# Attention and a two-layer network on one core: the first 700 items of a hand-written order rearranged

## The chip, the core and the metric

The kernel runs on one core of a Trainium2 chip. The core has five engines, each with its own in-order queue: TensorE (matmul, PE in the profile; its weight loads are PEld), VectorE (DVE), ScalarE (ACT), GpSimd (POOL) and SyncE (SP), which here only issues DMAs. They wait for one another through semaphores. TensorE writes into PSUM, which has 8 banks of 128 x 512 float32. The metric is the device time of one execution in microseconds (us).

## What is computed

Attention with causal masks over 4 batches, 8 heads, 768 positions and 64 columns per head. Three heads see all earlier positions; the other five see the first 4 positions and a window of 64. The result, as 3072 tokens of 512 columns, goes through two matrix products with a leaky rectifier between them.

```python
scores = scale * np.matmul(q, k.transpose(0, 1, 3, 2))
...
stream_keep = causal & (is_sink | in_win)
...
a = np.exp(scores)
a = a / (np.sum(a, axis=-1, keepdims=True) + 1e-09)
return np.matmul(a, v).astype(np.float32)
```

```python
h = x @ w_in
g = np.maximum(h, 0.0) + alpha * np.minimum(h, 0.0)
return (g @ w_out).astype(np.float32)
```

w_in is 512 x 2048, w_out is 2048 x 512; x is the attention's result, batch by batch.

## The kernel before

**Segments and blocks.** The heads go in pairs (2,6), (1,5), (0,4), (3,7); a pair of one batch is a segment, n = 0 to 15, four to a batch. The first four (batch 0) are the first stage. The tokens go through the network in eight groups, t = 0 to 7: of each batch 512 tokens (even t) and 256 (odd t).

**Items.** The program is a list of some 1,100 named items, ORDER, which line 807 emits one after another. An item is one step of one segment or block; its letter tells which, and its numbers the segment (n), the head of the pair (h) and the part:

- Lq, Lk, Lv n: loads of q, k and v, on SyncE (one load of k on ScalarE, one on GpSimd). Cq, Ck, Cv: casts to bfloat16, on GpSimd, VectorE or ScalarE as strings at line 296 and below say.
- Tq, Tk n: transposes on TensorE into PSUM; tq, tk n.h: copies from there into qT and kT (put_q, line 369; put_k, line 387 and below). From segment 8 on DMAs do this (Dq, Dk).
- S n.h.m: scores of one part (TensorE, line 414 in the first stage; from segment 4 on they are gathered in a group and issued at lines 424 or 431, the two heads side by side). s n.h.m: exponentials (ScalarE, lines 470, 518, 524). m n.h.m: masks (VectorE, lines 480, 529, 532).
- A n.h: product with v (TensorE, line 553); a n.h: reciprocal and scaling (VectorE, lines 563 and 564). X n and x n: transposes into xT, by TensorE and VectorE (lines 578 and 583) in segments 0 to 3 and 15, by DMA (line 572) in the others.
- P t.f: the first product, 128 x 512 values of one bank (TensorE, line 598); in t = 0, blocks f < 6, it comes in three parts, the first of which reads the pairs 0 and 1 of xT. p t.f: negated rectifier (ScalarE, line 603, three buffers); g t.f: the rectifier's sum (VectorE, line 610), which frees the bank.
- O t.s.u: a quarter of the second product (TensorE, line 618); o t.s: copy out of PSUM (ScalarE, line 624) and the output's DMA (GpSimd, line 628). L and l are the last tile of it, in three cuts.
- Fills and masks that are made once: ro, sz, so, near (constants in the tails of the exponentials' buffers), kz, qz, vz, vo, nz, kfz (line 288 in the profile), nmr, nms (masks of the first stage, on GpSimd), nr, ns, one, zero, busy, id. warm: matmuls on the tile busy, without a use of their result (line 688).
- wi, wo: loads of the weights, issued by GpSimd.

**What sets the order.** An engine executes its own instructions in the order of the list; between engines only the data order them. The place in the list decides one more thing: a step that needs a PSUM bank takes, of those that its kind may use, the one that was given back longest ago in the list (take and give, lines 144 and 150), and so waits for whoever gave it back. Scores of the first stage take the banks 0 and 1 or 2 and 3 in pairs; A, X and some transposes of the first stage take 6 or 7; most others any.

**Names in the prediction.** tk0.1 is the copy of the second head's keys of segment 0 into kT, in two pieces (put_k, line 387); S0.1.0, S0.1.1 and S0.1.2 are that head's scores, s0.1.x their exponentials, A0.0 and A0.1 the products with v of the two heads. ro0 fills the tail of the first buffer eR, which A0.0 and A0.1 read. near2 refills parts of the third buffer eS. x1 copies the second pair's transposes into xT. m9.0.2 is two instructions (lines 529 and 532). nz0 zeroes a buffer that Ck8 writes into; Cv5 and Cv4 are casts of v on GpSimd.

Of the kernel before, what the change touches and what calls it, by code (L numbers as in the profile page):

```python
# [11 lines left out]


ORDER = """
vz2 id busy warm4 warm0 warm5 vz0 qz0 Lq0.0 sz2 so2 Lq0.1 zero vz3 nms Lk1 Lq1 sz1 Cq0.1 nmr Ck1.1 kz1 La Lk0 Ck1.0
kz0 Cq1 Cq0.0 Tq0.0 Ck0.0 Tk0.0 tk0.0 Lk2 Ck2.0 Lv0 warm2 tq0.0 S0.0.0 s0.0.0 qz S0.0.1 Tk1 warm3 warm6 vo kz2 Ck0.1
vz1 Ck2.1 Tq1 s0.0.1 tq1 Tq0.1 tk1.1 S0.0.2 s0.0.2 Cv0 tk1.0 m4.0.2 warm7 tq0.1 Lq2 S1.1.0 Tk0.1 tk0.1 S1.0.0 ro0
s1.1.0 Tk2 tk2.1 idf Cq2 s1.0.0 S0.1.0 s0.1.0 A0.0 S0.1.1 s0.1.1 S0.1.2 Tq2 warm8 s0.1.2 tq2 S1.1.1 s1.1.1 A0.1 kz3
sz0 Lk3 Ck3.1 Lv1 S1.0.1 m4.1.2 a0.0 s1.0.1 Al Ck3.0 Lq3 tk2.0 Tk3 S2.0.1 s2.0.1 a0.1 tk3.1 al X0 x0 S2.0.2 Lv2 Lv3
so1 so0 Lq5 wi1 s2.0.2 Lk4 m8.0.2 wi0 Cq3 Tq3 S2.0.0 s2.0.0 tk3.0 Cv1 tq3 A1.0 a1.0 Lk5 kfz2 A1.1 a1.1 kfz0 S2.1.0  # L20
S2.1.1 Cv2 s2.1.1 kfz3 wi6 A2.0 a2.0 wi7 S3.1.0 s2.1.0 s3.1.0 wi5 wi4 S3.0.0 A2.1 Cv3.0 s3.0.0 X1 S3.1.1 s3.1.1 S3.0.1
a2.1 X2 x1 x2 m8.1.2 near2 Ck4.0 P0.0.0 wi2 s3.0.1 A3.0 Cv3.1 P0.3.0 a3.0 P0.2.0 P0.2.1 A3.1 Ck4.1 Lk7 Lk6 P0.1.0
P0.1.1 P0.0.1 Tk4 tk4.0 Cq5 m14.0.2 a3.1 X3 nz1 tk4.1 x3 Tq5 P0.3.1 tq5 P1.2 p1.2 P1.0 p1.0 g1.0 P0.1.2 wi3 P0.13 Lq4
one p0.1 g0.1 P0.2.2 Lq6 Lv7 p0.2 P0.0.2 P1.14 p1.14 g1.2 g1.14 Ck5.0 Ck5.1 nr Tk5 tk5.1 P0.3.2 tk5.0 g0.2 p0.0 g0.0
p0.3 g0.3 P0.12 p0.12 g0.12 p0.13 g0.13 P0.14 kfz1 P1.8 P0.8 wo0 p0.8 g0.8 P0.10 Ck7.1 S5.1.1 s5.1.1 P0.15 p0.15 wo1
wo2 wo3 ns p1.8 g0.15 g1.8 P0.11 p0.11 p0.14 g0.14 p0.10 S5.0.0 Lv5 P0.7 g0.10 P0.6 Ck6.1 P0.4.0 Lq7 P0.4.1 Lk8 Ck6.0
s5.0.0 p0.7 S5.0.2 s5.0.2 Cq4 Tq4 tq4 g0.11 P0.4.2 P0.9 nz0 Ck7.0 S5.1.0 p0.9 g0.9 P1.4 s5.1.0 p1.4 Lv6 S4.0.1 Cq6
m12.1.2 P0.5.0 s4.0.1 P0.5.1 P0.5.2 P1.12 m5.0.0 g1.4 S4.0.3 g0.7 p0.4 p0.5 m5.1.0 g0.4 g0.5 Cv5 P1.10 S5.0.1 p1.10
s5.0.1 near0 p0.6 g0.6 O0.1.0 Tq6 s4.0.3 m4.0.3 Tk6 tk6.1 tk6.0 O0.2.0 P1.6 p1.6 m5.0.1 Tk7 tk7.1 Lv4 S4.0.2 O0.2.1
g1.6 ro1 tq6 p1.12 s4.0.2 tk7.0 O0.1.1 O0.2.2 O0.1.2 g1.10 S4.0.4 S4.0.0 S5.1.2 g1.12 S4.0.5 S4.1.4 S4.1.0 s4.0.4  # L30
s4.0.0 m5.1.1 m4.0.4 s4.1.0 m4.1.0 m5.0.2 O0.1.3 s5.1.2 O0.3.0 O0.2.3 Cq7 m5.1.2 Ck8 Tq7 near1 A5.1 o0.1 S6.1.0 s4.1.4
s6.1.0 O0.3.1 a5.1 s4.0.5 O0.3.2 O0.3.3 m4.0.1 m4.0.5 Cv4 tq7 S7.0.0 S6.0.5 S7.1.1 S4.1.1 Lk9 Lk10 Lq9 o0.2 o0.3
S4.1.3 S7.0.1 A5.0 s4.1.1 s7.0.0 m4.0.0 a5.0 X5 A4.0 s7.0.1 Lk11 s7.1.1 a4.0 s4.1.3 O1.1.0 m4.1.3 Cv7 s6.0.5 m7.0.0
m7.1.1 Lq8 S7.1.0 S6.0.4 S7.0.2 S4.1.5 S6.0.1 S7.1.2 S6.1.1 O1.1.1 Cv6 s7.1.0 O1.0.0 s4.1.5 m7.0.1 s6.1.1 m4.1.5
m6.1.1 s7.1.2 m6.1.0 s7.0.2 m7.0.2 S6.0.2 S4.1.2 S6.1.2 S6.0.0 s6.0.4 s4.1.2 s6.0.1 s6.1.2 O1.0.1 m6.0.5 m7.1.0 m4.1.1
# [812 lines left out]
```

## Time and profile before

| | us |
|---|---|
| median of the runs (227.71, 228.17, 228.29) | 228.17 |
| the profiled execution | 228.43 |
| its span, first to last instruction | 225.8 |
| TensorE busy | 221.6 |
| VectorE busy | 149.1 |
| ScalarE busy | 140.1 |
| GpSimd busy | 45.9 |

By stretches of the span, from the view that sums them (busy time of TensorE, VectorE, ScalarE and GpSimd):

| stretch, us | what runs | TensorE | VectorE | ScalarE | GpSimd |
|---|---|---|---|---|---|
| 0 to 26 | loads, first stage | 24.63 | 20.29 | 18.47 | 18.63 |
| 26 to 53 | first blocks P, segments 4 and 5 | 27.00 | 19.89 | 22.62 | 13.65 |
| 53 to 80 | segments 4 to 7, products O | 27.00 | 18.26 | 18.27 | 3.49 |
| 80 to 120 | blocks of batch 1, segments 8 to 11 | 40.00 | 32.41 | 30.59 | 4.30 |
| 120 to 225.8 | the rest | 102.92 | 58.30 | 50.12 | 5.87 |

In the rows of a timeline the columns are the start, the duration, the engine, the line, the operation, what is written and read with the shape, the count, and in brackets the idle time of the engine before it and what ended that. Neighbours of one kind are merged into one row with their count. Matmuls are pipelined: a matmul's duration reaches past the start of the next one, so the distance between starts tells the pace, and a busy TensorE can hold short waits. In the view of waits, the columns are who waited for what, the time in total, the number of waits and the longest. The chain is the work that ended last, followed back through what released each step; a row of it has start, duration, engine, tile and line.

### The profile page before, as it was taken

Reading aid. Unit: us, or ns where it says so; the run is one execution under the profiler, and the core shown is the slowest. Engines: PE = TensorE matmul, PEld = TensorE weight load, DVE = VectorE, ACT = ScalarE, POOL = GpSimd, SP = SyncE. Lnnn points to the kernel's source line nnn. Section 1 sums busy time; section 2 is a strip of 40 time slices with the busy share of each in tenths; the row PEclk is TensorE's granted clock in tenths of the full one; section 3 lists DMA queues with packets and bytes.
Section 4 is the critical chain, followed back from the end, with each engine's and each line's share of the span. In section 5 each row is a group of like instructions: output and inputs, shape, how many; then the busy total and the mean of one; then the engine's idle time right before and its main releaser. Section 6 shows DMA issues by size and latency. Waiting matters only on the chain.

```text
span 225.8 us, 5241 instructions
## 1 busy us (share of the span) xinstructions
PE 221.6 (98%) x2005; PEld 136.5 (60%) x2005; DVE 149.1 (66%) x393; ACT 140.1 (62%) x286; POOL 45.9 (20%) x91
## 2 busy tenths in 40 slices
PE   7999999999999999999999999999999999999994
PEld 7989876575556557564556455456556555664454
DVE  5798648986659618897899029977486536866000
ACT  3788669999898036587992147786584237563311
POOL 5679749600230001000400001000110100000000
PEclk9999999999999999999999999999999999999999
DMA  6999999999999999999989999976924420000213
GB/s 201 311 240 214 281 223 285 197 196 231 204 284 182 117 232 231 170 167 190 268 160 177 226 243 129 238 156 117 119 94 38 120 93 0 0 3 1 93 68 119
DMA packets 95417, 37.39 MB, mean 166 GB/s; under 512 B 82440, under 2 KB 93600, under 8 KB 95392
## 3 DMA queue, kind: packets, MB, share of 16 engines
q1 hardware_dynamic: 89136, 27.73, 65.2%
q0 software_dynamic: 5792, 8.93, 17.5%
q10 hardware_dynamic: 464, 0.40, 0.6%
q8 instruction: 15, 0.25, 0.5%
q14 instruction: 10, 0.08, 0.1%
HBM read 27.71 MB, written 6.29 MB: 151 GB/s over the span
## 4 chain that ended last, share of the span: by engine, by line
PE 98%; DVE 0%; issue 0%; DVEq 0%
PE P L598 37%; PE P L618 36%; PE P L553 7%; PE P L431 4%; PE P L414 3%; PE P L688 3%; PE P L364 2%; PE P L637 2%; PE P L424 1%; PE P L502 1%; PE P L578 1%; PE P L463 0%; PE P L362 0%; DVE kT L387 0%; DVE ot L646 0%
## 5 line engine op out<-in xcount | busy, mean ns | idle before, releaser
L610 DVE SCALAR_TENSOR_TENSOR g<-neg,oma,P 128x256 bf16<-128x256 f32 (+1 forms) x128 | 70.9, 608 | 36.9 <-ACT neg L603 36.4
L598 PE MATMUL P<-xT,w_in_b 128*128 128x512 bf16 (+1 forms) x512 | 86.6, 326 | 0.0
L618 PE MATMUL P<-w_out_b,g 128*128 128x512 bf16 x368 | 85.3, 379 | 0.0
L603 ACT ACTIVATE neg<-P 128x512 f32<-128x512 f32 x96 | 54.2, 600 | 26.3 <-PE P L598 20.9
L598 PEld LDWEIGHTS <-w_in_b 128*128 128x128 bf16 x512 | 49.5, 98 | 32.3 <-DVE g L610 0.2
L618 PEld LDWEIGHTS <-g 128*128 128x128 bf16 x368 | 33.9, 98 | 37.2 <-issue 1.0
L470 ACT ACTIVATE eR<-P 128x448 bf16<-128x448 f32 (+4 forms) x63 | 36.9, 635 | 5.8 <-PE P L431 2.5
L624 ACT COPY ot<-P 128x512 f32<-128x512 f32 x23 | 13.9, 605 | 37.1 <-PE P L618 32.3
L628 POOL DMA_DIRECT2D out_dram<-ot x18 | 10.3, 572 | 111.0 <-ACT ot L624 110.8
L518 ACT ACTIVATE eS<-P 128x352 bf16<-128x352 f32 x45 | 20.8, 489 | 3.4 <-PE P L431 3.0
L564 DVE TENSOR_TENSOR xn<-P,rcp 128x448 bf16<-128x448 f32 (+1 forms) x32 | 19.5, 608 | 1.1
L529 DVE TENSOR_TENSOR eS<-eS,ms_near 128x352 bf16<-128x352 bf16 x45 | 14.9, 346 | 0.6 <-ACT eS L518 0.5
L563 DVE RECIPROCAL rcp<-P 128x7 f32<-128x7 f32 (+1 forms) x32 | 6.3, 198 | 10.9 <-PE P L553 10.8
L480 DVE TENSOR_TENSOR eR<-eR,mr_near 128x128 bf16<-128x128 bf16 (+5 forms) x54 | 10.7, 227 | 4.3 <-ACT eR L470 4.1
L414 PE MATMUL P<-qT,kT 128*128 128x192 bf16 (+14 forms) x68 | 11.2, 251 | 0.2 <-DVE kT L387 0.2
L553 PEld LDWEIGHTS <-eS 128*128 128x128 bf16 x260 | 9.5, 97 | 2.3 <-issue 0.6
L553 PE MATMUL P<-vb,eS 128*128 128x65 bf16 x260 | 10.7, 193 | 0.0
L431 PE MATMUL P<-qT,kT 64*128 64x176 bf16 (+10 forms) x168 | 10.5, 252 | 0.0
L431 PEld LDWEIGHTS <-kT 64*128 64x128 bf16 x168 | 6.7, 94 | 6.2 <-issue 5.5
L553 PE MATMUL P<-vb,eR 128*128 128x65 bf16 x276 | 10.5, 193 | 0.0
L553 PEld LDWEIGHTS <-eR 128*128 128x128 bf16 x276 | 9.5, 97 | 1.3
L646 DVE COPY ot<-P 128x128 f32<-128x128 f32 x1 | 0.3, 291 | 14.3 <-PE P L637 14.3
(95 smaller groups left out, 177.3 us busy)
## 6 DMA issues: line engine op xcount, KB each, us to landing
out_dram<-ot POOLq DMA_DIRECT2D x18, 256.0 KB, 3.9
kf<-in_k_dram SPq DMA_DIRECT2D x21, 192.0 KB
qf<-in_q_dram SPq DMA_DIRECT2D x18, 192.0 KB
vf<-in_v_dram SPq DMA_DIRECT2D x14, 196.0 KB
qf<-in_q_dram SPq DMA_DIRECT2D x7, 384.0 KB
vf<-in_v_dram SPq DMA_DIRECT2D x12, 192.0 KB
w_in_b<-in_moe_w_in_dram POOLq DMA_DIRECT2D x8, 256.0 KB, 9.6
w_out_b<-in_moe_w_out_dram POOLq DMA_DIRECT2D x4, 512.0 KB, 13.9
```

Of the source, the lines that this page charges most:

```text
L414: nc.tensor.matmul(to, keys, queries, start=True, stop=stop)
L431: nc.tensor.matmul(to, keys[own], queries[own], start=True, stop=True)
L470: nc.scalar.activation(ebuf[n, hh][:, lo:hi].rearrange("p (x c) -> p x c", x=len(parts)), P[:, got[0]:got[0] + len(parts), 0:(hi - lo) // ...
L518: nc.scalar.activation(slots, sc[:, 0:352].rearrange("p (s c) -> p s c", c=176), AF.Exp, scale=scale)
L529: nc.vector.tensor_tensor(slots, slots, ms_near[:, 0:2, :] if m == 0 else ms_near[:, 1:3, :], op=ALU.mult)
L553: nc.tensor.matmul(pav[:, i, :], e[:, o:o + 128], vv[:, j, hh, 0:D + 1], start=(m == 0), stop=(m == len(terms) - 1))
L564: nc.vector.tensor_tensor(xn[n][:, 0:nt, D * hh:D * hh + D], pav[:, :, 0:D], rcp.to_broadcast([128, nt, D]), op=ALU.mult)
L598: nc.tensor.matmul(psg[:, w * i:w * (i + 1)], w_in_b[:, c, 128 * fb:128 * (fb + 1)], xT[:, c, o:o + w], start=(x == 0), stop=(x == 3))
L603: nc.scalar.activation(neg[t, f], bank(held["P", t, f][0]), AF.Relu, scale=-1.0)
L610: nc.vector.scalar_tensor_tensor(g_buf[t % 2][:, fb, 0:w], neg[t, f][:, c], oma[:, fb:fb + 1], bank(got[0])[:, c], op0=ALU.mult, op1=ALU.add)
L618: nc.tensor.matmul(bank(held["O", t, s][0]), g_buf[t % 2][:, f, 128 * s:128 * (s + 1)], w_out_b[:, f, :], start=(f == 0), stop=(f == 15))
L624: nc.scalar.copy(ot, bank(got[0]))
```

## The change

ORDER is replaced. The first 700 names stand in a new order, and the last 376 are as they were; no name is added or dropped, and no function changes. Below are the lines that hold what the prediction speaks of; the lists wrap at other places.

```diff
--- before.py
+++ after.py
...
 
 ORDER = """
-vz2 id busy warm4 warm0 warm5 vz0 qz0 Lq0.0 sz2 so2 Lq0.1 zero vz3 nms Lk1 Lq1 sz1 Cq0.1 nmr Ck1.1 kz1 La Lk0 Ck1.0
-kz0 Cq1 Cq0.0 Tq0.0 Ck0.0 Tk0.0 tk0.0 Lk2 Ck2.0 Lv0 warm2 tq0.0 S0.0.0 s0.0.0 qz S0.0.1 Tk1 warm3 warm6 vo kz2 Ck0.1
-vz1 Ck2.1 Tq1 s0.0.1 tq1 Tq0.1 tk1.1 S0.0.2 s0.0.2 Cv0 tk1.0 m4.0.2 warm7 tq0.1 Lq2 S1.1.0 Tk0.1 tk0.1 S1.0.0 ro0
-s1.1.0 Tk2 tk2.1 idf Cq2 s1.0.0 S0.1.0 s0.1.0 A0.0 S0.1.1 s0.1.1 S0.1.2 Tq2 warm8 s0.1.2 tq2 S1.1.1 s1.1.1 A0.1 kz3
...
-S2.1.1 Cv2 s2.1.1 kfz3 wi6 A2.0 a2.0 wi7 S3.1.0 s2.1.0 s3.1.0 wi5 wi4 S3.0.0 A2.1 Cv3.0 s3.0.0 X1 S3.1.1 s3.1.1 S3.0.1
-a2.1 X2 x1 x2 m8.1.2 near2 Ck4.0 P0.0.0 wi2 s3.0.1 A3.0 Cv3.1 P0.3.0 a3.0 P0.2.0 P0.2.1 A3.1 Ck4.1 Lk7 Lk6 P0.1.0
...
-s5.0.0 p0.7 S5.0.2 s5.0.2 Cq4 Tq4 tq4 g0.11 P0.4.2 P0.9 nz0 Ck7.0 S5.1.0 p0.9 g0.9 P1.4 s5.1.0 p1.4 Lv6 S4.0.1 Cq6
-m12.1.2 P0.5.0 s4.0.1 P0.5.1 P0.5.2 P1.12 m5.0.0 g1.4 S4.0.3 g0.7 p0.4 p0.5 m5.1.0 g0.4 g0.5 Cv5 P1.10 S5.0.1 p1.10
...
-s6.1.0 O0.3.1 a5.1 s4.0.5 O0.3.2 O0.3.3 m4.0.1 m4.0.5 Cv4 tq7 S7.0.0 S6.0.5 S7.1.1 S4.1.1 Lk9 Lk10 Lq9 o0.2 o0.3
...
-a6.0 O1.1.3 O0.0.0 O0.0.1 O0.0.2 O1.0.2 m10.0.2 O1.0.3 O0.0.3 o0.0 X4 X6 a7.1 a7.0 X7 P2.9 P2.3 p2.9 P3.4 Ck9 Cq9 g2.9
-P2.14 p2.14 g2.14 Cq8 p3.4 Lq10 Lq11 Dk8.0 P2.10 p2.10 Dk9.1 o1.0 p2.3 g2.3 g3.4 Dk8.1 P3.2 P3.14 P3.12 P2.8 Dq8 P2.1
-P3.8 o1.1 p3.2 Dk9.0 Lv10 g2.10 Dq9 p3.14 P2.7 Ck10 g3.2 p3.12 g3.12 g3.14 P2.2 p2.2 g2.2 Cq10 Dq10 P2.11 p2.1 g2.1
-p2.11 p2.8 g2.11 P3.6 P2.5 p2.5 g2.5 P2.13 p2.13 g2.8 g2.13 P2.0 p2.0 g2.0 p2.7 P3.0 p3.0 P2.4 S8.0.5 Lv8 Lv11 P2.15
...
-s9.0.2 p3.8 P3.10 g3.8 p3.10 O3.0.0 O2.0.0 S8.1.5 s8.1.5 O3.0.1 O2.0.1 g3.10 m8.0.0 Cv8 S8.1.3 S9.0.0 S8.0.3 S9.1.1
-S8.0.1 S9.1.0 s8.1.3 s9.1.0 s8.0.1 s9.0.0 s8.0.3 m8.0.3 m8.0.1 O2.0.2 O2.0.3 o2.0 Dk10.1 Lv9 m9.0.0 Cv9 m8.0.5 Dk11.0
-m9.1.0 m9.0.2 S8.0.4 S9.0.1 S10.1.1 S8.1.4 Dq11 s8.1.4 Lq13 Lk13 O3.0.2 Dk10.0 s9.1.1 s10.1.1 s9.0.1 s8.0.4 O3.0.3
...
-O2.2.0 O2.1.0 s10.0.4 m6.0.2 m10.0.1 Cv11 m8.1.1 m8.1.0 a10.1 m10.0.4 Ck13 m10.0.0 m11.1.2 A11.0 A8.1 O2.1.1 s10.0.2
...
+vz2 id busy warm0 warm4 warm5 vz0 qz0 Lq0.0 sz2 so2 Lq0.1 Lk1 Lq1 zero nmr vz3 sz1 nms Cq0.1 Ck1.1 kz1 La Lk0 Ck1.0
+kz0 Cq1 Cq0.0 Tq0.0 Ck0.0 Tk0.0 tk0.0 Lk2 warm2 Ck2.0 Lv0 tq0.0 S0.0.0 s0.0.0 qz S0.0.1 Tk1 warm3 kz2 vo Ck0.1 warm6
+vz1 Ck2.1 Tq1 s0.0.1 tq1 tk1.1 S0.0.2 s0.0.2 Cv0 tk1.0 m4.0.2 Tq0.1 Lq2 tq0.1 warm7 S1.1.0 Tk0.1 ro0 S1.0.0 s1.1.0
+tk0.1 Tk2 tk2.1 Cq2 S0.1.0 idf s1.0.0 s0.1.0 S0.1.1 s0.1.1 A0.0 S0.1.2 warm8 Lk3 Tq2 s0.1.2 S1.1.1 tq2 s1.1.1 A0.1 kz3
...
+s2.1.0 S2.1.1 s2.1.1 kfz3 wi6 A2.0 S3.1.0 wi7 wi5 S3.0.0 a2.0 s3.1.0 wi4 A2.1 s3.0.0 Cv3.0 X1 S3.1.1 s3.1.1 S3.0.1
+a2.1 X2 near2 x1 x2 m8.1.2 Ck4.0 P0.0.0 wi2 s3.0.1 A3.0 P0.3.0 P0.2.0 a3.0 Ck4.1 Cv3.1 P0.2.1 A3.1 Lk7 m14.0.2 Lk6
...
+P0.5.0 Cq6 P0.5.1 P1.12 m5.1.0 P0.5.2 m5.0.0 g1.4 S4.0.3 g0.7 s4.0.1 p0.4 g0.4 p0.5 g0.5 Cv5 P1.10 p1.10 S5.0.1 s5.0.1
+near0 p0.6 g0.6 O0.1.0 nz0 Tq6 s4.0.3 Tk6 tk6.1 m4.0.3 tk6.0 O0.2.0 P1.6 Lv4 p1.6 m5.0.1 Tk7 S4.0.2 s4.0.2 tk7.1 g1.6
...
+O0.3.1 a5.1 s4.0.5 O0.3.2 o0.2 m4.0.5 O0.3.3 Cv4 tq7 m4.0.1 S4.1.1 S6.0.5 S7.0.0 Lk9 Lk10 S4.1.3 S7.1.1 S7.0.1 A5.0
...
+a6.0 O0.0.1 O1.0.2 m10.0.2 O1.0.3 O0.0.2 O0.0.3 o0.0 X4 X6 a7.1 a7.0 X7 P2.3 Cq9 P2.1 P2.9 Ck9 P2.14 p2.9 g2.9 p2.14
+g2.14 Cq8 P3.4 Lq10 Lq11 P2.10 p3.4 p2.10 Dk8.0 Dk9.1 Dk8.1 o1.0 P3.14 p2.3 g2.3 P3.2 g3.4 P3.12 P2.8 Dq8 P3.8 o1.1
+p3.2 Dk9.0 Lv10 g2.10 Dq9 p3.14 P2.7 Ck10 p3.12 g3.12 P2.2 g3.14 p2.2 g3.2 Cq10 g2.2 Dq10 P2.11 p2.1 g2.1 p2.8 p2.11
+g2.8 g2.11 P2.5 p2.5 g2.5 P2.13 p2.13 g2.13 P2.0 p2.0 g2.0 p2.7 P3.0 p3.0 P2.4 S8.0.5 Lv8 Lv11 P2.15 P2.12 s8.0.5 Cq11
+g3.0 p2.15 g2.7 g2.15 S8.0.0 p2.12 g2.12 Ck11 s8.0.0 P3.6 p3.6 S9.0.2 P2.6 p2.6 g3.6 g2.6 p2.4 g2.4 s9.0.2 p3.8 P3.10
+m9.0.2 g3.8 p3.10 O3.0.0 O2.0.0 S8.1.5 s8.1.5 O3.0.1 g3.10 O2.0.1 m8.0.0 m8.0.5 Cv8 S8.1.3 S8.0.3 S9.0.0 S9.1.1 S8.0.1
+S9.1.0 s8.1.3 s8.0.1 s9.0.0 s8.0.3 s9.1.0 m8.0.3 m8.0.1 O2.0.2 O2.0.3 m9.0.0 o2.0 Dk10.1 Lv9 Cv9 Dk11.0 m9.1.0 S8.0.4
...
+m10.0.1 m6.0.2 Cv11 m8.1.0 m8.1.1 a10.1 s10.0.4 A8.1 m10.0.4 Ck13 m11.1.2 A11.0 s10.0.2 o2.3 s11.1.0 m10.0.0 Dk13.0
...
```

Read by engine, this changes the following. SyncE issues the same DMAs in the same order. GpSimd: nmr before nms, Cv5 before nz0, o0.2's DMA before Cv4. ScalarE: s2.1.0 before s2.1.1, p1.2 after p1.0 and p0.1, s4.0.2 directly after p1.6, o0.2 before tq7, and some six more of this kind. VectorE: ro0 before tk0.1, a0.0 before sz0, so1 and so0 before x0, near2 before x1, g0.2 before g1.2 and g1.14, m5.1.0, m8.0.5, m9.0.2 and m9.1.1 earlier, m4.1.0, m7.0.0, g3.2 and others later. TensorE: S0.0.2 before Tq0.1, S0.1.1 before A0.0, warm8 before Tq2, P1.14 and P1.12 one part earlier, O0.0.0 before A7.0, the blocks P2 and P3 from 80 us on in another order (P2.3, P2.1, P2.9, P2.14, P3.4, P2.10, P3.14, P3.2, P3.12, P2.8 in place of P2.9, P2.3, P3.4, P2.14, P2.10, P3.2, P3.14, P3.12, P2.8, P2.1), P3.6 after S8.0.0, A8.1 before A11.0, and scores inside their groups.

## The prediction

> **What bounds the kernel now.** I read the page's busy shares and the chain that ended last, then the waits of TensorE, then its timeline.
>
> ```profile
> PE 221.6 (98%) x2005; PEld 136.5 (60%) x2005; DVE 149.1 (66%) x393; ACT 140.1 (62%) x286; POOL 45.9 (20%) x91
> ...
> PE 98%; DVE 0%; issue 0%; DVEq 0%
> ```
>
> ```profile
> PE P L414 <- DVE kT L387: 0.2, 1, 0.2
> ```
>
> ```profile
> 79.21 1.03 PE L618 MATMUL P<-w_out_b,g 128*128 128x512 bf16 x4
> 80.07 11.87 PE L598 MATMUL P<-xT,w_in_b 128*128 128x512 bf16 x74
> ```
>
> The chain is TensorE from end to end, and the view of waits finds, beside the start, one idle time of it: 0.2 us before a score (line 414). A busy TensorE need not be dense, so look at starts: the four matmuls of 79.21 are followed by the next group at 80.07, 0.86 us later, which is 215 ns for 512 columns. A stream as dense as this gains nothing from another order. What an order can do is remove or add waits, and they lie in the first stage, where TensorE, VectorE and ScalarE hand small pieces to each other:
>
> ```profile
> 12.02 0.50 PE L364 MATMUL P<-ident,g 128*128 128x128 bf16 x6
> 12.69 0.36 PE L414 MATMUL P<-qT,kT 128*128 128x448 bf16 x1 [0.17 <-DVE kT L387]
> ...
> 13.19 0.80 PE L553 MATMUL P<-vb,eR 128*128 128x65 bf16 x21
> 13.82 0.54 PE L414 MATMUL P<-qT,kT 128*128 128x448 bf16 x3
> 14.20 0.22 PE L463 MATMUL P<-nmr,ident 128*128 128x128 bf16 x1
> 14.36 0.35 PE L414 MATMUL P<-qT,kT 128*128 128x128 bf16 x2
> ...
> 14.91 0.50 PE L364 MATMUL P<-ident,g 128*128 128x128 bf16 x6
> ...
> 15.81 0.96 PE L553 MATMUL P<-vb,eR 128*128 128x65 bf16 x21
> 16.61 0.24 PE L414 MATMUL P<-qT,kT 128*128 128x192 bf16 x1
> ```
>
> In order these are Tk2, S0.1.0, A0.0, S0.1.1 (two rows), S0.1.2, Tq2, A0.1 and S1.0.1. Six 128-column matmuls in 0.50 us, the last one lasting 0.22, start 56 ns apart. So Tk2's last start is 12.30, and S0.1.0 at 12.69 comes 0.33 us late. S0.1.2 comes 0.10 late (14.20 to 14.36, less 0.06). A0.0 and A0.1 are alike, but the starts of A0.0 span 0.63 us (13.19 to 13.82) and those of A0.1 0.80 (15.81 to 16.61): 0.17 of wait inside. Together 0.6 us, against a bound of 0.3% (0.68 us), which is about what a measurement of this kernel can tell from no change.
>
> **The change, part by part.** The order is read engine by engine. SyncE issues the same DMAs in the same order, ScalarE's two DMAs of the start are where they were, and TensorE has the same 2005 matmuls; the groups of scores from segment 4 on hold the same items, some in another order inside. So TensorE's work is unchanged, and the sum is one of waits.
>
> *ro0 ahead of tk0.1 (VectorE, first stage).* This memset of eR's tail now stands before the copy for which S0.1.0 waits.
>
> ```profile
> 11.32 0.96 DVE L369 COPY qT<-P 64x768 bf16<-64x768 bf16 x1
> 12.20 1.03 DVE L387 COPY kT<-P 64x258 bf16<-64x258 bf16 x2
> 13.33 0.20 DVE L288 MEMSET eR<- 128x164 f32 x1
> 13.54 0.94 DVE L393 COPY kT<-P 64x744 bf16<-64x744 bf16 x1
> ```
>
> ```profile
> 12.20 0.43 DVE kT L387
> ```
>
> ```profile
> 13.39 0.92 ACT L470 ACTIVATE eR<-P 128x896 bf16<-128x896 f32 x1 [0.36 <-PE P L463]
> 14.46 1.73 ACT L470 ACTIVATE eR<-P 128x896 bf16<-128x896 f32 x2 [0.15 <-PE P L463]
> ```
>
> VectorE runs without a pause here (tq0.1, tk0.1, ro0, tk2.1). The memset costs 0.21 start to start, 0.10 between tk0.1's end (13.23) and its start, and the 0.08 by which tk0.1 now overlaps tq0.1 (12.28 to 12.20): 0.39 us. The first piece of tk0.1 ends at 12.63 + 0.39 = 13.02, and S0.1.0 starts at 13.07. The order after it is S0.1.0 (0.50), S0.1.1 (now ahead of A0.0; 13.82 to 14.26, 0.44) and A0.0 (0.63): 13.57, 14.01, 14.64. The second piece, ready at 13.62, is wanted by the third matmul of S0.1.1 at 13.79: no wait. S0.1.2 needs the banks that s0.1.0 frees: 14.31 + 0.39 = 14.70, so it starts at 14.75, again 0.39 later than before. Then the wait in A0.1 goes: it is for s0.1.2, which ended at 14.46 + 1.73 = 16.19. S0.1.2 ended at 15.07 (0.06 before Tq2's start, plus 0.22), now at 15.46; s0.1.2 takes 0.92, to 16.41; the ninth matmul of A0.1 is due at 15.81 + 0.39 + 0.27 = 16.47. So 0.39 - 0.17 = **0.22 us later** at S1.0.1. What follows to 26 us is paced by TensorE's own output through the copies of VectorE, so I see nothing that takes it back. Bounds: 0.21 - 0.17 = 0.04, if only the start-to-start cost counts, and 0.39.
>
> *near2 ahead of x1 (VectorE).*
>
> ```profile
> 25.15 0.55 DVE L583 COPY xT<-P 128x768 bf16<-128x768 bf16 x1
> ...
> 26.41 0.10 DVE L682 MEMSET eS<- 128x48 f32 x1
> 26.46 0.09 DVE L683 MEMSET eS<- 128x32 f32 x1
> ```
>
> ```profile
> 25.69 0.59 PE L598 MATMUL P<-xT,w_in_b 128*128 128x512 bf16 x2
> ```
>
> Two memsets, 0.14 together, and x1 ends at 25.84 in place of 25.70. The second matmul of P0.0.0 reads it at 25.69 + 0.22 = 25.91. Between 0 and 0.14; I take 0.05, for the time from an end to a start.
>
> *P2.3 and P2.1 ahead of P2.9 (TensorE, 80 us), p2.3 and p2.1 where they were.* Each of the two holds a bank longer, and the later ones come round sooner.
>
> ```profile
> 81.13 0.60 ACT L603 ACTIVATE neg<-P 128x512 f32<-128x512 f32 x1 [0.28 <-PE P L598]
> ...
> 85.18 0.61 ACT L624 COPY ot<-P 128x512 f32<-128x512 f32 x1
> 85.64 0.64 ACT L603 ACTIVATE neg<-P 128x512 f32<-128x512 f32 x1
> ```
>
> ```profile
> 86.32 0.75 DVE L610 SCALAR_TENSOR_TENSOR g<-neg,oma,P 128x512 bf16<-128x512 f32 x1 [0.74 <-ACT neg L603]
> ```
>
> Blocks take 0.865 us; p2.9 started 1.06 after its block. P2.10 is now sixth, at 84.40, so p2.10 is at 85.46; o1.0 and p2.3 follow at the pace of 85.18 to 85.64, 0.46 each, at 85.92 and 86.38, g2.3 0.68 after p2.3 (85.64 to 86.32), from 87.06 to 87.81. Following the banks through the new order, P2.8, tenth, takes g2.3's bank at 87.85 (80.07 + 9 x 0.865). Before, g2.3 ended at 87.07 and its bank went to a later block. Bounds 0 and 0.3 (o1.0 and p2.3 after p2.10 without the overlap of 0.15 that each shows: 85.18 + 0.61 against 85.64); I take 0.05.
>
> *m9.0.2 ahead of g3.8 and g3.10 (VectorE, 104 us).*
>
> ```profile
> 102.33 2.98 DVE L610 SCALAR_TENSOR_TENSOR g<-neg,oma,P 128x512 bf16<-128x512 f32 x6
> ```
>
> ```profile
> 105.22 0.71 PE L431 MATMUL P<-qT,kT 64*128 64x176 bf16 x12
> ```
>
> ```profile
> 59.18 0.34 DVE L529 TENSOR_TENSOR eS<-eS,ms_near 128x352 bf16<-128x352 bf16 x1
> ...
> 59.55 0.62 DVE L334 CAST natk<-kf 128x896 bf16<-128x896 f32 x1
> ```
>
> Such a mask is two instructions, and the one at 59.18 leaves the engine to the next work at 59.55: 0.37. g3.10, which ended at 105.31, ends at 105.68, and frees the bank of S9.1.0, last in the group that starts at 105.22 and is issued over some 0.4 us. Between 0 and 0.37; I take 0.10.
>
> *At nothing.* nz0 now waits behind Cv5 on GpSimd, and o0.2's output DMA goes ahead of Cv4:
>
> ```profile
> 42.42 0.89 POOL L288 MEMSET natk<- 128x960 f32 x1
> 56.30 0.93 POOL L349 CAST vb<-vf 128x896 bf16<-128x896 f32 x1 [13.00 <-DMA vf<-in_v_dram]
> ```
>
> ```profile
> 62.76 0.93 POOL L349 CAST vb<-vf 128x896 bf16<-128x896 f32 x1 [1.55 <-DMA vf<-in_v_dram]
> 63.63 0.56 POOL L628 DMA_DIRECT2D out_dram<-ot  x1
> ```
>
> ```profile
> 64.71 0.80 PE L553 MATMUL P<-vb,eR 128*128 128x65 bf16 x21
> ```
>
> nz0 ends at 57.23 + 0.89 = 58.12, and its reader Ck8 starts at 59.55: 1.4 us of cover. If v5's load is later than that, VectorE stands at Ck8 with near1 and a5.1 behind it. Cv4 ends 0.56 later, at 64.25, and A4.0 reads it at 64.71. The remaining moves (nmr with nms, vo, sz0, x0, s2.1.0, p1.2, P1.14, P1.12, s4.0.2, A7.0, A8.1, g2.8, P3.6 and the scores inside their groups) pass neighbours, and P3.6 seven blocks, with the same sum of work before the next reader that TensorE waits for; 0 to 0.1 for all, taken as 0.
>
> **Sum:** 0.22 + 0.05 + 0.05 + 0.10 = 0.42 us, on the traced execution's 228.43: 228.85. That execution stands 0.26 over the median of the runs shown, 228.17, so the median to expect is **228.6**. Lowest and highest sums: 0.04 and 0.39 + 0.14 + 0.30 + 0.37 = 1.20.
>
> **Rivals.**
>
> *Loads that come later than traced (faster).*
>
> ```profile
> 11.06 0.93 POOL L349 CAST vb<-vf 128x896 bf16<-128x896 f32 x1 [1.02 <-DMA vf<-in_v_dram]
> ```
>
> Cv0 waits for v0's load and ends at 11.99, 1.20 before A0.0. In the new order A0.0 starts at 14.01, 2.02 after it. An execution whose v0 is over 1.2 late loses up to 0.82 less: 228.17 - 0.82 = 227.35. For it: the four times lie between 227.71 and 228.43, so something varies. Against it: that spread is no larger than 0.72, and in the trace no load ends a wait of TensorE.
>
> *VectorE is the bound wherever it is given something earlier (slower).* The mechanism is one in-order queue without slack: what is put ahead is paid in full, from the point where the cover is shorter than the inserted work: ro0 0.39, near2 0.14, m9.0.2 0.37. Sum 0.90: 228.17 + 0.90 = 229.1. For it: no idle time of VectorE around tk0.1. Against it: 66% busy over the span, and A0.1's wait, which takes up part.
>
> *TensorE's clock falls in the longer wait (slower).*
>
> ```profile
> 1.21 4.45 PE L688 MATMUL P<-busy 128*128 128x128 bf16 x40 [1.21 <-DVE busy L288]
> ```
>
> The first 40 matmuls take 111 ns each, those of Tq2 56. The wait before S0.1.0 becomes 0.33 + 0.39 = 0.72 us; if that sends the array back to the slow pace for as many matmuls, it costs 40 x 55 ns = 2.2 us: 230.4. Against it: the 0.33 us of before left the next ones at 56 ns. The Trainium skill (TensorE: Matmul & The Clock Gate, Part 1: The HAM clock gate) says the array falls back to half its clock after an idle window of about 3.4 us; by that rule 0.72 us is too short, and the trace so far agrees.
>
> *Nothing changes.* The waits only move: 228.2.
>
> **How the numbers follow.** Forecast as summed 0.42; nothing 0.12; late loads 0.15; VectorE the bound 0.28; the clock 0.03. The first two lie within 0.3% (227.49 to 228.85): same 0.54. Faster 0.15, slower 0.31. The predicted time is 228.6. The range goes from the late loads' 227.4 to 229.5, over VectorE's case, since the upper sum of 1.20 would give 229.4; it leaves out the clock and the ends of the others. The forecast's own range is 228.2 to 229.0.
>
> **What would show it.** In the new profile: ro0 before tk0.1, and TensorE idle before line 414 for 0.4 to 0.6 us where it was 0.17; A0.1's starts spanning 0.63; S1.0.1 about 0.2 later than 16.61; P2.8 and S9.1.0 starting within 0.1 of the end of the g before them; from 26 us to the end the same distances as before. I am wrong if the first stage ends earlier than before, if TensorE shows a wait after 30 us that was not there, or if the whole difference is in DMA landings.

## The result, and the profile after

| | before | after |
|---|---|---|
| median of six runs each, us | 227.94 (227.52 to 228.36) | 229.99 (229.38 to 230.53) |
| the profiled execution, us | 228.43 | 229.84 |
| its span, us | 225.8 | 228.1 |

The ratio is 1.009, with a 95% interval from 1.0069 to 1.0112: slower by 1.6 to 2.6 us. The forecast was 228.6, and its range ended at 229.5. Here and below a time is the median of the runs, and the ratios leave out the few runs of a slower state (233.07 us at a granted clock of 0.993, for one), which the ranges of the times include.

The view of TensorE's waits after the change shows what is new. Its columns are who waited for what, the time in total, the number of waits and the longest.

```profile
PE P L688 <- DVE busy L288: 1.2, 1, 1.2
PE P L414 <- DVE kT L387: 1.1, 1, 1.1
PE P L414 <- ACT eS L524: 0.6, 1, 0.6
```

Before, line 414 waited once, for 0.2 us. Now it waits twice. TensorE's timeline after the change says where (start, duration, engine, line, operation, and in brackets the idle time and who ended it).

```profile
5.58 1.30 PE L362 MATMUL P<-ident,g 128*64 128x128 bf16 x12
6.81 0.95 PE L688 MATMUL P<-busy 128*128 128x128 bf16 x14
...
12.42 0.50 PE L364 MATMUL P<-ident,g 128*128 128x128 bf16 x6
13.47 0.36 PE L414 MATMUL P<-qT,kT 128*128 128x448 bf16 x1 [0.56 <-ACT eS L524]
...
16.60 0.80 PE L553 MATMUL P<-vb,eR 128*128 128x65 bf16 x21
17.24 0.24 PE L414 MATMUL P<-qT,kT 128*128 128x192 bf16 x1
...
17.84 0.51 PE L364 MATMUL P<-ident,g 128*128 128x128 bf16 x6
19.46 0.57 PE L414 MATMUL P<-qT,kT 128*128 128x455 bf16 x3 [1.12 <-DVE kT L387]
...
20.15 0.51 PE L578 MATMUL P<-ident,xn 128*128 128x128 bf16 x6
```

The rows are Tq0.0 with Tk0.0, warm2, Tk2, S0.1.0, A0.1, S1.0.1, Tk3, S2.0.1 and X0. The same part of the trace of before, as far as the prediction did not show it:

```profile
5.58 0.90 PE L362 MATMUL P<-ident,g 128*64 128x128 bf16 x12
6.42 0.96 PE L688 MATMUL P<-busy 128*128 128x128 bf16 x14
...
17.21 0.51 PE L364 MATMUL P<-ident,g 128*128 128x128 bf16 x6
17.55 0.56 PE L414 MATMUL P<-qT,kT 128*128 128x455 bf16 x3
...
18.00 0.50 PE L578 MATMUL P<-ident,xn 128*128 128x128 bf16 x6
```

Read downwards, the difference of the starts grows in three places. At warm2 it is 0.39 us (6.42 to 6.81), and the change has no part in it: the twelve transposes ahead of it take 1.30 us in place of 0.90, since TensorE's slow pace of the start lasted longer in this execution. At S0.1.0 it is 0.78 (12.69 to 13.47), 0.39 of which is new; at S1.0.1 0.63, so 0.15 came back in A0.1. At S2.0.1 it is 1.91 (17.55 to 19.46), and at X0 2.15: between S1.0.1 and X0, which are 1.39 us apart before, 1.52 us were lost, more than all that the prediction added up. By A2.0 it is 2.28 (21.63 to 23.91), and there it stays: P0.1.0 goes from 27.98 to 30.27, S9.1.0 from 105.58 to 107.86, L0 from 219.95 to 222.23.

The 0.39 at S0.1.0 is ro0's: VectorE's timeline after the change has it (line 288, eR) ahead of tk0.1.

```profile
12.76 0.20 DVE L288 MEMSET eR<- 128x164 f32 x1
12.99 1.03 DVE L387 COPY kT<-P 64x258 bf16<-64x258 bf16 x2
```

What S2.0.1 waits for is VectorE's copy tk2.0 (line 387). Further on in the same timeline, the row of line 288 that writes eS is sz0:

```profile
15.53 0.56 DVE L564 TENSOR_TENSOR xn<-P,rcp 128x384 bf16<-128x384 f32 x1
18.39 0.22 DVE L288 MEMSET eS<- 128x192 f32 x1 [2.30 <-ACT eS L524]
18.52 0.89 DVE L387 COPY kT<-P 64x768 bf16<-64x768 bf16 x1
19.33 0.17 DVE L563 RECIPROCAL rcp<-P 128x6 f32<-128x6 f32 x1
19.54 0.56 DVE L564 TENSOR_TENSOR xn<-P,rcp 128x384 bf16<-128x384 f32 x1
20.13 0.94 DVE L393 COPY kT<-P 64x744 bf16<-64x744 bf16 x1
```

and before, with ScalarE's row that ends with s1.0.1 behind it (two instructions of 384 columns: s1.1.1, which writes the second buffer eS, and s1.0.1, which writes the first):

```profile
14.85 0.22 DVE L288 MEMSET eS<- 128x192 f32 x1
15.10 0.20 DVE L563 RECIPROCAL rcp<-P 128x6 f32<-128x6 f32 x1
15.32 0.56 DVE L564 TENSOR_TENSOR xn<-P,rcp 128x384 bf16<-128x384 f32 x1
15.80 0.94 DVE L387 COPY kT<-P 64x768 bf16<-64x768 bf16 x1
...
17.85 0.94 DVE L393 COPY kT<-P 64x744 bf16<-64x744 bf16 x1 [0.25 <-PE P L364]
```

```profile
16.75 0.91 ACT L524 ACTIVATE eS<-P 128x384 bf16<-128x384 f32 x2
```

sz0 is a memset of 0.22 us. Before, it ran at 14.85, ahead of a0.0 (reciprocal and scaling), and VectorE went on without a pause to tk2.0 at 15.80, 1.75 us ahead of S2.0.1. After, VectorE stands idle for 2.30 us at sz0, until ScalarE has ended line 524. The row of ScalarE after the change has the same two instructions at 17.39 for 0.89, so s1.0.1 ends at 18.28, and sz0 starts at 18.39. Behind sz0 in VectorE's queue stand tk2.0 (18.52), a0.1 (19.33 and 19.54) and tk3.1 (20.13, line 393). S2.0.1 waits for the first of them. X0 reads the second, which ends at 20.10, and starts at 20.15; that is where the difference grows from 1.91 to 2.15.

The chain of waits of that stretch, in order of time, runs through exactly these (start, duration, engine, tile, line):

```profile
17.50 0.79 ACT eS L524 x2
18.29 0.10 issue
18.39 0.22 DVE eS L288
18.60 0.81 DVE kT L387
19.42 0.05 issue
19.46 0.57 PE P L414 x3
```

The list shows what changed. These lines of the diff are the ones that the prediction passed over:

```diff
-sz0 Lk3 Ck3.1 Lv1 S1.0.1 m4.1.2 a0.0 s1.0.1 Al Ck3.0 Lq3 tk2.0 Tk3 S2.0.1 s2.0.1 a0.1 tk3.1 al X0 x0 S2.0.2 Lv2 Lv3
+Ck3.1 Lv1 a0.0 S1.0.1 s1.0.1 m4.1.2 Al Ck3.0 sz0 Lq3 tk2.0 Tk3 S2.0.1 s2.0.1 a0.1 tk3.1 al X0 S2.0.2 Lv2 Lv3 so1 so0
```

sz0 moved from ahead of s1.0.1 to behind it. Both write the first buffer eS: sz0 the columns 192 to 255 of each of its six slots of 256 columns, s1.0.1 the columns 0 to 191 of slots 4 and 5. They share no element. But the stretch from the first to the last column that one of them writes reaches into that of the other. That these stretches set the wait is the theory that the experiments try.

### The profile page after: what moved, and what is told of

It is laid out like the page before. It is cut to its first block, busy times and chain, and to the rows that moved or that the text cites. A ratio compares the mean times of both kernels' runs of the same rounds, so it can differ in the third digit from the quotient of the medians.

```text
span 228.1 us, 5209 instructions
## 1 busy us (share of the span) xinstructions
PE 220.7 (97%) x1977; PEld 136.9 (60%) x2005; DVE 148.3 (65%) x393; ACT 140.6 (62%) x286; POOL 46.8 (21%) x91
## 3 DMA queue, kind: packets, MB, share of 16 engines
HBM read 27.71 MB, written 6.29 MB: 149 GB/s over the span
## 4 chain that ended last, share of the span: by engine, by line
PE 93%; DVE 2%; ACT 2%; issue 1%; DVEq 0%
PE P L598 36%; PE P L618 35%; PE P L553 6%; PE P L431 4%; PE P L688 3%; PE P L364 2%; PE P L414 2%; PE P L637 2%; PE P L424 1%; DVE kT L393 1%; ACT eR L470 1%; PE P L502 1%; ACT eS L524 1%; PE P L578 1%; PE P L362 1%
## 5 line engine op out<-in xcount | busy, mean ns | idle before, releaser
L598 PE MATMUL P<-xT,w_in_b 128*128 128x256 bf16 (+1 forms) x502 | 85.8, 325 | 0.5
L618 PE MATMUL P<-w_out_b,g 128*128 128x512 bf16 x350 | 83.5, 379 | 1.0
L529 DVE TENSOR_TENSOR eS<-eS,ms_near 128x352 bf16<-128x352 bf16 x45 | 14.3, 334 | 2.2 <-ACT eS L518 2.1
L431 PE MATMUL P<-qT,kT 64*128 64x176 bf16 (+11 forms) x168 | 10.6, 251 | 0.0
```

The source lines that it names most:

```text
L431: nc.tensor.matmul(to, keys[own], queries[own], start=True, stop=True)
L529: nc.vector.tensor_tensor(slots, slots, ms_near[:, 0:2, :] if m == 0 else ms_near[:, 1:3, :], op=ALU.mult)
L598: nc.tensor.matmul(psg[:, w * i:w * (i + 1)], w_in_b[:, c, 128 * fb:128 * (fb + 1)], xT[:, c, o:o + w], start=(x == 0), stop=(x == 3))
L618: nc.tensor.matmul(bank(held["O", t, s][0]), g_buf[t % 2][:, f, 128 * s:128 * (s + 1)], w_out_b[:, f, :], start=(f == 0), stop=(f == 15))
```

## The experiments

The theory (A): sz0 behind s1.0.1 in the list waits for it, because their stretches overlap, and holds up tk2.0 in VectorE's queue. The rivals: loads and casts that come at other times (B), a wait that only moves when it is taken away (C), the blocks and masks from 80 us on (D), that any place of sz0 behind s1.0.1 costs as much (E), and that the whole buffer, not a stretch of it, sets the wait (F). Beside them stands the prediction's own ro0. For all runs the table at the end of this section gives the distances in TensorE's timeline from warm2 on, since they are free of the start's pace.

**sz0 back, in the new order.**

```diff
-Ck3.1 Lv1 a0.0 S1.0.1 s1.0.1 m4.1.2 Al Ck3.0 sz0 Lq3 tk2.0
+Ck3.1 Lv1 a0.0 sz0 S1.0.1 s1.0.1 m4.1.2 Al Ck3.0 Lq3 tk2.0
```

> The changed order with one name moved: sz0 (VectorE's memset of the gaps in the first buffer eS) again ahead of S1.0.1 and s1.0.1 in the list. Theory A (in the list sz0 stands behind s1.0.1, whose range of addresses reaches across its columns, so VectorE waits for that exponential with tk2.0 and a0.1 behind it): VectorE's 2.3 us of idle time before the memset goes, S2.0.1 follows Tk3 without the 1.1 us wait, and the time falls by 1.5 us, to 0.4 us over before. Rival B (the wait of S2.0.1 comes from the first stage's loads and the later start of everything, and sz0 only happens to stand there): VectorE waits at tk2.0 or a0.1 instead, and the time stays 2.0 us over before.

228.20 us (227.15 to 229.81, 12 runs) against 227.92 before; ratio 1.0013 [0.9983, 1.0042]. One name put back takes the loss away as far as the times can tell. In VectorE's timeline of this kernel sz0 and tk2.0 follow a0.0 without a pause:

```profile
14.86 0.56 DVE L563 TENSOR_TENSOR xn<-P,rcp 128x384 bf16<-128x384 f32 x1
15.40 0.22 DVE L287 MEMSET eS<- 128x192 f32 x1
15.54 0.89 DVE L386 COPY kT<-P 64x768 bf16<-64x768 bf16 x1
```

The other 699 places are those of the changed kernel, so its loads (B), its blocks and its masks (D) are no cause of the loss.

**sz0 late, in the old order.**

```diff
-sz0 Lk3 Ck3.1 Lv1 S1.0.1 m4.1.2 a0.0 s1.0.1 Al Ck3.0
+Lk3 Ck3.1 Lv1 S1.0.1 m4.1.2 a0.0 s1.0.1 sz0 Al Ck3.0
```

> The order of before with one name moved: sz0 directly behind s1.0.1 in the list; on VectorE it then stands behind a0.0, as in the changed order. Theory A: VectorE stands at sz0 until s1.0.1 has ended (17.65 in the trace of before, against 14.85 for the memset), tk2.0 ends some 1.9 us later than 16.74, S2.0.1 waits for it, and the time rises by 1.2 to 1.6 us. Rival B: the same time as before, within 0.2 us.

229.27 us (228.93 to 229.51, 6 runs) against 227.92; ratio 1.006 [1.0037, 1.0083]. The move alone makes the old kernel slower, by 0.8 to 1.9 us. VectorE's timeline has the wait again, with the same releaser:

```profile
15.08 0.56 DVE L563 TENSOR_TENSOR xn<-P,rcp 128x384 bf16<-128x384 f32 x1
17.71 0.22 DVE L287 MEMSET eS<- 128x192 f32 x1 [2.07 <-ACT eS L523]
17.84 0.89 DVE L386 COPY kT<-P 64x768 bf16<-64x768 bf16 x1
```

**sz0 and ro0 back, in the new order.** As the first, and ro0 behind tk0.1.

```diff
-warm7 S1.1.0 Tk0.1 ro0 S1.0.0 s1.1.0 tk0.1 Tk2 tk2.1
+warm7 S1.1.0 Tk0.1 S1.0.0 s1.1.0 tk0.1 ro0 Tk2 tk2.1
```

> The changed order with two names moved back: sz0 ahead of S1.0.1, and ro0 behind tk0.1. Theory A with the prediction's term for ro0 (0.39 us at S0.1.0, 0.16 of it given back in A0.1): 0.2 us under the kernel with sz0 alone moved back, so 0.1 to 0.3 us over before, and S0.1.0 waits 0.33 us as before. Rival C (ro0 costs nothing in the end, since the wait only moves): the same time as with sz0 alone moved back.

227.89 us (227.07 to 233.07, 12 runs) against 227.92; ratio 1.0004 [0.9984, 1.0024]. The times can't tell it from the first; the trace can. From warm2 to S0.1.0 it is 6.29 us with ro0 behind tk0.1 and 6.66 with ro0 ahead of it, so ro0 costs 0.37. It also settles an ambiguity of the profile: the row of S0.1.0 after the change names ScalarE as what ended its wait, because s1.0.0 ended at that very moment (13.43). That engine wasn't moved here, and the wait went with ro0; it had been for tk0.1: with ro0 back S0.1.0 starts at 12.43, and s1.0.0 ends only at 13.10. In this execution L0 is 0.90 us late on top: k5's load came late, the cast Ck5.1 waited for it, and Tk5 after it. No other profiled execution shows that.

**The old order up to P0.0.0 (161 names), the new one from there.**

```diff
-vz2 id busy warm0 warm4 warm5 vz0 qz0 Lq0.0 sz2 so2
...
-S3.0.1 a2.1 X2 near2 x1 x2 m8.1.2 Ck4.0
+vz2 id busy warm4 warm0 warm5 vz0 qz0 Lq0.0 sz2 so2
...
+S3.0.1 a2.1 X2 x1 x2 m8.1.2 near2 Ck4.0
 P0.0.0 wi2 s3.0.1 A3.0 P0.3.0
```

> The order of before up to P0.0.0, and all other names in the changed order. Theory A puts the whole loss into the first stage: the time of before within 0.2 us, and from 26 us on the same distances between matmuls as before. Rival D (the prediction's small terms for P2.8 and S9.1.0, and the bank that P2.1 holds): 0.15 to 0.8 us over before, with TensorE late at P2.8 or S9.1.0.

228.01 us (227.06 to 229.86, 12 runs) against 227.92; ratio 1.0011 [0.9984, 1.0037]. From warm2 to L0 it is 213.53 us, to the hundredth what it is before. All the rest of the 700 items, with the blocks and masks for which the prediction had put 0.05 and 0.10, costs nothing in the trace; the runs alone would allow up to 0.8 us.

**sz0 still later: behind a0.1.**

```diff
-Ck3.0 sz0 Lq3 tk2.0 Tk3 S2.0.1 s2.0.1 a0.1 tk3.1
+Ck3.0 Lq3 tk2.0 Tk3 S2.0.1 s2.0.1 a0.1 sz0 tk3.1
```

> The changed order with sz0 moved further back in the list, from before tk2.0 to behind a0.1. Theory A: the memset still has to wait for s1.0.1, but only tk3.1 is behind it on VectorE, and a0.1 and s1.0.1 end together (17.19 and 17.24 in the kernel with sz0 moved back), so the wait costs under 0.1 us: the time of that kernel, 0.3 to 0.4 us over before. Rival E (not the place on VectorE but any place behind s1.0.1 costs, for instance because the readers of eS are then later): 1.3 us or more over before.

227.89 us (227.34 to 229.4, 12 runs) against 227.82; ratio 1.0013 [0.9993, 1.0033]. Here too sz0 stands behind s1.0.1 and is released by it, but what stands behind sz0 is not urgent:

```profile
15.64 0.94 DVE L386 COPY kT<-P 64x768 bf16<-64x768 bf16 x1
16.94 0.20 DVE L562 RECIPROCAL rcp<-P 128x6 f32<-128x6 f32 x1 [0.36 <-PE P L552]
17.17 0.56 DVE L563 TENSOR_TENSOR xn<-P,rcp 128x384 bf16<-128x384 f32 x1
17.89 0.22 DVE L287 MEMSET eS<- 128x192 f32 x1 [0.16 <-ACT eS L523]
```

The wait is 0.16 us in place of 2.30. So E falls: the price isn't that of the wait as such, but of what is queued behind it. Only tk3.1 is here, and it starts 0.16 us later than with sz0 back (18.14 less 6.31, against 17.45 less 5.78, each counted from warm2).

**sz0 in six pieces, one of them ahead of S1.0.1.** The six memsets cover the same columns, a slot each; slot 4's stands ahead of S1.0.1, the other five where the change put sz0.

```diff
+    for s_ in range(6):
+        fill(f"sz0_{s_}", eSv[:, 0, s_, 192:SLOT].bitcast(fp32), 0.0)
...
-a0.0 S1.0.1 s1.0.1 m4.1.2 Al Ck3.0 sz0 Lq3 tk2.0
+a0.0 sz0_4 S1.0.1 s1.0.1 m4.1.2 Al Ck3.0 sz0_0 sz0_1 sz0_2 sz0_3 sz0_5 Lq3 tk2.0
```

> The changed order with sz0 cut into six memsets, one for each gap of 64 columns. s1.0.1 writes the slots 4 and 5 (columns 0 to 191 of each), so from its first to its last column only the gap of slot 4 lies inside. That memset goes ahead of S1.0.1, the other five stay where sz0 is in the changed order. Theory A in the form that a wait is set for ranges from first to last column: no wait for s1.0.1, and the time of the kernel with sz0 moved back or up to 0.4 us more, for five more small memsets. Rival F (the wait is set for the whole buffer): VectorE waits at the first of the five for s1.0.1, as in the changed order, 1.8 to 2.2 us over before.

228.34 us (227.36 to 229.72, 12 runs) against 227.82; ratio 1.0014 [0.9981, 1.0047]. Five of the six stand behind s1.0.1 in the list, one of them in a slot that s1.0.1 writes, and none waits for it. VectorE's and ScalarE's timelines:

```profile
15.78 0.56 DVE L563 TENSOR_TENSOR xn<-P,rcp 128x384 bf16<-128x384 f32 x1
16.29 0.29 DVE L287 MEMSET eS<- 128x32 f32 x6
16.50 0.91 DVE L386 COPY kT<-P 64x768 bf16<-64x768 bf16 x1
```

```profile
17.58 0.89 ACT L523 ACTIVATE eS<-P 128x384 bf16<-128x384 f32 x2
```

The pieces are done at 16.58; s1.0.1, the second of the two instructions in ScalarE's row, ends it at 18.47, so the pieces did not wait for it. Slot 5's piece begins one column behind the last one that s1.0.1 writes. So it is neither the buffer (F) nor the slot that decides; the stretch from the first to the last column fits all the places tried. The opposite test, slot 4's piece behind s1.0.1, where by this rule it would wait, was not run.

**Two tries for a gain.** The wait of 0.33 us before S0.1.0, which is in the old kernel too, is VectorE's: a memset of 0.81 us, kz2, stands ahead of tk1.1. First it was moved back in the old order, from ahead of tk1.1 to ahead of tk2.1.

```diff
-warm6 vo kz2 Ck0.1
+warm6 vo Ck0.1
...
-s1.1.0 Tk2 tk2.1 idf
+s1.1.0 Tk2 kz2 tk2.1 idf
```

> The order of before with one name moved: kz2, a memset of 0.81 us on VectorE, from ahead of tk1.1 to ahead of tk2.1, behind tk0.1. By the prediction's reading of the first stage (S0.1.0 waits 0.33 us for tk0.1, and VectorE runs without a pause up to it) tk1.1 can start at the end of Tk1, some 0.3 us earlier, and S0.1.0's wait goes: 0.2 to 0.35 us under before. Rival C (the wait only moves, to a place that needs ScalarE or tk2.1): the same time as before.

227.95 us (227.64 to 229.0, 12 runs) against 227.82; ratio 1.0014 [0.9995, 1.0032]. The wait before S0.1.0 went, and 0.24 us with it. VectorE's timeline shows where it came back:

```profile
13.66 0.20 DVE L287 MEMSET eR<- 128x164 f32 x1
14.00 0.81 DVE L287 MEMSET kT<- 128x896 f32 x1
14.90 0.94 DVE L392 COPY kT<-P 64x744 bf16<-64x744 bf16 x1
...
17.42 0.94 DVE L386 COPY kT<-P 64x768 bf16<-64x768 bf16 x1
```

tk2.0, which ran 9.38 us behind warm2 before (15.80 less 6.42), now runs 10.41 behind it (17.42 less 7.01), S2.0.1 waits for it, and at A2.0 the kernel is 0.64 us later: here the wait moved (C), and cost more in its new place. Then kz2 was given to GpSimd, directly ahead of Cv0:

```diff
-    for i in (0, 1, 2):
+    for i in (0, 1):
         fill(f"kz{i}", kT_all[:, i].bitcast(fp32), 0.0)
+    fill("kz2", kT_all[:, 2].bitcast(fp32), 0.0, nc.gpsimd)
...
-S0.0.2 s0.0.2 Cv0
+S0.0.2 s0.0.2 kz2 Cv0
```

> The kernel before, with the memset kz2 (0.81 us on VectorE, ahead of tk1.1) given to GpSimd, directly ahead of Cv0, where GpSimd stood 1.02 us idle for v0's load. Nothing is computed otherwise. In before_kz2_late the distance from warm2 to S0.1.0 was 6.03 us in place of 6.27, so the wait ahead of S0.1.0 had gone, but VectorE paid the memset again ahead of tk2.1, and at A2.0 the kernel was 0.64 us later. Theory (the order costs where an engine is handed work ahead of what TensorE waits for): with the memset off VectorE altogether, warm2 to S0.1.0 is 6.03 again, and the 0.24 stays: X0 11.3 to 11.4 us behind warm2 (before 11.58), A2.0 15.0 (15.21); S2.0.1 without a wait. The median 0.2 to 0.3 us under the kernel before's, about 0.999, which the runs alone can't tell from no change; the trace decides. Rival (the wait only moves): the first distance is 6.03, and the 0.24 is lost again by A2.0, because S1.0.1 to A2.0 is set by ScalarE's exponentials; the median as before. Rival (GpSimd is late): v0's cast Cv0 is held up by the memset, A0.0 waits for it, and S1.0.1 is later than 10.19 behind warm2.

227.57 us (227.31 to 229.12, 12 runs) against 227.95; ratio 0.9989 [0.9961, 1.0018]. In the trace the wait before S0.1.0 is gone and does not come back, and 0.33 us, somewhat more than expected, stay won to the end (6.27 to 5.94 at S0.1.0, 213.53 to 213.19 at L0). GpSimd's timeline shows the cover, the idle time ahead of the cast of v0:

```profile
10.59 0.85 POOL L288 MEMSET kT<- 128x896 f32 x1
11.37 0.94 POOL L349 CAST vb<-vf 128x896 bf16<-128x896 f32 x1
```

It is the lowest of the medians and distances, but 0.33 us of 228 is less than these runs can tell from no change.

Distances from warm2, us, each the difference of two starts in TensorE's timeline of the profiled execution:

| kernel | S0.1.0 | S1.0.1 | X0 | A2.0 | L0 |
|---|---|---|---|---|---|
| before | 6.27 | 10.19 | 11.58 | 15.21 | 213.53 |
| after | 6.66 | 10.43 | 13.34 | 17.10 | 215.42 |
| after, sz0 back | 6.66 | 10.43 | 11.82 | 15.45 | 213.77 |
| before, sz0 late | 6.27 | 10.20 | 13.11 | 16.86 | 215.18 |
| after, sz0 and ro0 back | 6.29 | 10.18 | 11.57 | 15.20 | 214.43 (k5 late) |
| old stage, new rest | 6.27 | 10.20 | 11.60 | 15.22 | 213.53 |
| after, sz0 behind a0.1 | 6.66 | 10.43 | 11.82 | 15.60 | 213.92 |
| after, sz0 in pieces | 6.66 | 10.43 | 11.82 | 15.45 | 214.02 |
| before, kz2 late | 6.03 | 9.95 | 12.10 | 15.85 | 214.17 |
| before, kz2 on GpSimd | 5.94 | 9.86 | 11.25 | 14.88 | 213.19 |

The two causes add up. sz0 alone costs 215.18 - 213.53 = 1.65 us, ro0 with what A0.1 gives back 213.77 - 213.53 = 0.24, together 1.89, and that is what the changed kernel shows: 215.42 - 213.53. The medians differ by 2.05, and the interval (1.6 to 2.6) holds 1.89. VectorE's rows tell why the loss lasts. From tk3.1 on VectorE has no pause up to a1.0, and A2.0 takes the bank that a1.0 gives back (a1.0 ends at 21.57 before and at 23.86 after), so A2.0 comes 3.78 us behind tk3.1 before (17.85 to 21.63) and after (20.13 to 23.91). What lasts is thus the delay of tk3.1, third behind sz0 in the queue; the 0.12 to 0.15 us by which A2.0 falls further behind X0 in four of the kernels is part of it. One small end stays open: the 0.25 us that the kernel with the six pieces loses near 25 us.

## Why the prediction was wrong, step by step

**The step that failed** is the last one "at nothing": "The remaining moves (nmr with nms, vo, sz0, x0, s2.1.0, ...) pass neighbours, ...; 0 to 0.1 for all, taken as 0." sz0 was read on VectorE alone, where it does pass one neighbour, a0.0. In the whole list it also passed S1.0.1 and s1.0.1, which run on other engines, and s1.0.1 writes the same buffer. Behind the failure stands the reading "engine by engine" and the sentence ahead of the prediction that between engines only the data order them: two instructions without a shared element were ordered here, by their stretches. Once the wait is known, rows give its cost. s1.0.1 ends before the change at 16.75 + 0.91 = 17.66, sz0 can't start ahead of that, tk2.0 follows 0.13 later (as in 18.39 to 18.52) at 17.79 and takes 0.94, to 18.73, and S2.0.1 comes at about 18.8 in place of 17.55. The kernel before with sz0 late has it at 18.79. The runs put the whole term at 1.65 us, where the prediction had 0.

**ro0** was right in mechanism and size: forecast 0.39 at S0.1.0, with 0.17 given back in A0.1 and 0.22 left; the changed kernel shows 0.39 and 0.24 left (6.66 and 10.43 against 6.27 and 10.19), and A0.1's starts span 0.64 us (16.60 to 17.24) where 0.63 was said. What follows did not take it back, as the prediction said. The move bought nothing: by the kernel's code ro0 fills the columns from 2728 on, while A0.0 and A0.1 read two different buffers eR, each up to column 2688; the first reader of what ro0 fills is A2.0.

**near2, P2.8 and S9.1.0**, forecast at 0.05, 0.05 and 0.10, cost nothing. x1 runs 0.10 us later than the shift of 2.28 explains (25.15 to 27.53), but P0.1.0 moves by 2.29. P2.8 starts at 90.19, and the tenth block of this stretch is due at 82.38 + 9 x 0.865 = 90.17. S9.1.0 moves by 2.28. In each of the three a cost between two bounds was taken a little above the lower one; the lower one was right.

**The rivals.** Late loads: a late load does occur (k5, in one trace), but the two orders do not differ by it, since the new order with sz0 back is no faster than the old. VectorE as the bound "wherever it is given something earlier": VectorE did become the bound, but by an instruction that was put later and waited, not by work put ahead; of that rival's three prices only ro0's was paid. TensorE's clock: after the wait of 1.12 us, longer than the 0.72 that was feared, X0's six transposes take 0.51 us where they took 0.50, so the clock stayed. Of the signs named for a wrong forecast none came: the first stage ended later, not earlier, no new wait of TensorE lies behind 30 us, and the DMAs have no part. The first signs named for a right one did come (the wait ahead of line 414 is 0.56 us, A0.1 spans 0.64). But no sign of either kind looked between S1.0.1 and A2.0, where the loss arose.

## What to carry to other kernels

When an instruction moves in a list that sets the waits, read what it passes on all engines, not only on its own, and for each one passed compare the stretches that the two touch, from the first to the last element, gaps included; in this kernel that told every wait that was tried. A fill of the gaps between strided pieces belongs ahead of whoever writes the pieces, or has to be cut so that no stretch of it reaches into theirs. The price of such a wait is what stands behind it in its engine's queue: the same late memset cost 1.65 us with tk2.0, a0.1 and tk3.1 behind it and 0.15 with tk3.1 alone.

## What the runs showed of the hardware

The start's slow pace ends at another moment in each execution. The twelve transposes at 5.58 took 0.90 us in the trace of before and 1.30 in that of after; in the trace with kz2 on GpSimd they took 1.44:

```profile
5.58 1.44 PE L362 MATMUL P<-ident,g 128*64 128x128 bf16 x12
```

The 40 matmuls ahead of these took 4.45 us before and after and 3.80 in the kernel with sz0 back. warm2 started anywhere between 5.78 and 7.01 us in the ten traces, whatever the order, and the shift stays to the end. That is 1.2 us, five times what ro0 costs; it may be a reason why runs of one kernel lie so far apart, but only one run of each has a trace. The Trainium skill (TensorE: Matmul & The Clock Gate, Part 1: The HAM clock gate) says that the gate looks at a free-running window, so that the moment at which it opens varies from run to run; by that rule the difference is no property of the order, and the traces agree: warm2 starts between 6.15 and 7.01 in the five with the old order of the first stage, and between 5.78 and 7.01 in the five with the new one.

An instruction on GpSimd took three times as long in the new order, with the same work. The third instruction of nms, an affine select of 192 columns, took 0.34 us in the old order:

```profile
3.06 0.34 POOL L272 TENSOR_SCALAR_AFFINE_SELECT nms<-nms 128x192 bf16<-128x192 bf16 x1
```

and 1.12 us behind nmr, as the change has it:

```profile
3.84 1.12 POOL L272 TENSOR_SCALAR_AFFINE_SELECT nms<-nms 128x192 bf16<-128x192 bf16 x1
```

It was 1.12 in the five traces with nmr first, and 0.34 or 0.35 in the five with nms first. Its cause is open: VectorE fills kT from 2.81 to 4.56, and so beside the short one at 3.06 as well as the long one at 3.84. TensorE lost nothing by it: with sz0 and ro0 back, the kernel has nmr first and the distances of before up to A2.0, within 0.02 us.
